# Causal block attention and a gated FFN on one core: a third piece with seven quarter products, plain maxima over the scores, low words on GpSimd

## The chip, the core and the metric

The kernel runs on one core of a Trainium2 chip. The metric is the device time in microseconds. Three runs of the kernel before took 951.97, 952.34 and 953.7 us; the median is 952.34.

## The reference

```python
scores = scale * np.matmul(q, k.transpose(0, 1, 3, 2))     # scale = 1/8
mask = block_i >= block_j                                  # blocks of 64 positions
scores = np.where(mask, scores, -1000000000.0)
scores = scores - np.max(scores, axis=-1, keepdims=True)
attn = np.exp(scores)
attn = attn / (np.sum(attn, axis=-1, keepdims=True) + 1e-09)
x = np.matmul(attn, v)                                     # heads side by side: 4608 x 512
...
h = x @ w_in                                               # 512 x 2048
g = h * np.clip(h + 3.0, 0.0, 6.0) / 6.0
out = g @ w_out                                            # 2048 x 512
```

There are 8 batches, 8 heads, 576 positions and head size 64; all inputs and outputs are float32.

## The kernel before

**Words.** A float32 operand is split into a high and a low float16 word (`nc.scaled` makes the high word, a multiply and subtract the low one), and a product is three float16 products: high x high, high x low, low x high. TensorE works with 64 output rows per matmul, two of them side by side on the two halves of the array.

**Attention.** Two heads make a pair (n = 0 to 31). Pairs 0 to 3 are computed in float32. For the others `s_group(n, g)` handles three blocks of 64 query rows (g = 0 to 2): it writes the scores of a block and all its keys into a bank of PSUM (`s`), and `to_softmax` lets VectorE copy the bank with a negative factor into the SBUF tile `p` and find the row minimum on the way, in one custom instruction and one that reads its accumulator. ScalarE takes the exponential of `p` in place, with the row sums; `st` holds minima, sums and their reciprocals. Then the high word of `p` times the reciprocal goes to `phl` on ScalarE or VectorE, and its low word by a `scalar_tensor_tensor` on VectorE (lines 1147 to 1158). A transposing DMA brings `phl` to `pT`, which `pv_group` multiplies with the words of V. Three PSUM buffers of tag s are shared by scores, pv and small statistics.

**FFN.** The 4608 tokens are cut into 13 pieces of at most 384 columns (numbers 0 to 12). A piece takes 16 slices f: the first layer makes h, ScalarE and VectorE make g from it, and the second layer adds g times `wout` into PSUM (`o`). In pieces of `STR` (line 56) the first layer is computed by a fast scheme with seven products of quarter matrices instead of eight (`h_pair`); it needs sums and differences of weights, made once by `w_comb`, and of x (`x_comb`). In pieces of `SO` (line 57) the second layer works so too (`g_pair`, `o_pair`); `t_comb` makes its tables once, from tiles `tr` and `tw` into room found by `t_homes`.

**Order.** Nothing here waits its turn by source order. `Recorder` collects every operation with its alternatives (`nc.add` gets a list of engines), and `ORDER`, a packed table of numbers, gives the order in which they are issued and the engine of each; `SLOTS` picks the buffer of each tile. So all instructions of an engine run in the order of the table, and they all carry line 423 in the profile.

Of the kernel before, what the change touches and what calls it, by code (L numbers as in the profile page):

```python
# [8 lines left out]
F16 = mybir.dt.float16  # L9
# [8 lines left out]
P = 128  # L18
# [38 lines left out]
SO = (11, 12)  # L57
# [21 lines left out]
    "c-l>Q1zaNC_qQS{Dvi0Rlyrl-X(u3IZra_oZrk0pZg+QgcXxMpcmL02pWpj=hvCLK-#GWqAk3~ghHbra)#^2C*O9O`!>rbC*obr4"  # L79
    "w0Vnj|A7Nsx&4S@9@%rSRK{}m=ZF-13Bha7)@|GUhQtT#*tu)BKrXaZdF<J{Z-2spgNF_uIeP54Hk^XD96G#NucI1#VuM3{$BY;i"  # L80
    "5_aO`Deu!~lxNSKpM2pWEi0mUT=o>Ry!??pqYDe#OG=9(qsPW|PBlg~#i-|Ns+RXz(9w5MbyrZJU3Xi>!j{&=X*KIMY_xDoN-it6"
    "uU)Y+r=f92@9tG~d#2OJ?@UQuJ!9sq1B^|(DsyjK-^bj0@Xgz_{p+_m9JzhxmZQ_L#cK{7Upsrw&A)iUw_o44o1HoP;OB(j=kDIS"
    "|IYj<?cv134)*7%pDui!g!yu%{_5t-Ted#?<7ja)<Lmot>6aXa`#gW~(s#+yWv{$n{~%HP1BhhLz|8)0Kj3Wq9KCFvoLxRTNoDdr"
    "%oBEx1`Qsn7?7C2QU(rmb#{wa(XnjzbcUrzT;r*er^gjO>DzDe<KQeIZ(hbzX;8A2yi_)9{Df@dip-{vi4ny`lSCzA375kcj2L-1"
    "yt!snN?zoU(PL&NrRuKaF3K+m3SOL+6Qv*97CmL<{#h}x#|*RU8>cF+wzMv3Dk~2?6BZJ>blLj$Yj9z%AFrrXTZeUYEmv!%byjWI"
    "xUaXmc4GJQIdwe^FQ(5RpW0Msd*Y<#*YC-v56pd7f8of{M}I!S#ku(S$-zUD{@yS%zZC!F^1P>*&u_ZppS_yDdyn?(%eSjn^{h!q"
    "tf^gVadVvw*0O=Q?e&ijtgTx%Z~tcXJ*oMpQpI-POQE&2PPx_g&Vyrzx4!$)v%lBy0WJjMxbc18Pw(SaI$_Yv+jj;J={NM=Fr2qG"
    "ynT6xD}BbS`?@nLR!+;!Ti_2xFv<qTC2)OL`S=Cs4J4}l&fY7DNduEp@^@V=C`_KWJ2Gm%vGYj!)Yxka7aYsHe)M>GT2WTTNKxgO"
    "(WAx|Z@jd5OE#~nx@6Pkh#_B7_w3F1CXBgoaRh($n(Ys|POe>dVr%qc!M^XaML$lZ9yoY<$DFx`4*&f1`_Hzaw}dxtzFGM8_WBKf"
    "@8sMZzxeLGclRGWd=#+=!^*aQe?4cyB))(vUXnW?udhp=e*Gia_5lN3-Ja~%m^p}-axVEsNou5${DMMj*|3RE-Q_%6bEfJ@R&^+j"  # L90
    "estM0ONR0j!OrTr4W2mI&yz&H@!{C#j~*MNhkH{TMmv7-qFxCIeDQM7V4v8Ac`>j2gI;f{RV)}Y_QVK_;E*t<ku>McqvF;#rZnqU"
    "zJm{It6?TKE#0YU@~zu-Tc%9Cvm?V#tJ_*s_UiK5%q#Pc-(5GZ{N968r_Y>SAO5i7@}tU@KlN1`+8#eS_t$LaQ+07xfAjko-1%MY"
    "nR_idW?6J%ySgt~O_<m-X)@OG!o}X{HYaVLS<g8-W%typv-eo`wd=PJPw=#|rta^5;2_bfWYA!m@1ZzK{ITOF7Lu}aj6R2t40-+L"
# [12 lines left out]
    "Dk2lFU#wbmv%2O|ZR5%rO*2<rKC^Jmjqd(E7B_G09yV+C$L8~O0^yuJb1$5|a<x7qbHVD(+=GYiUO&8d?bfX99A55?dGq(Fm3eEA"
    "jEvG~Z{0q+<yg2_)N=36fm0IQ1HBY(>y5;Rk0wohy#M4-BR@(e|N3IG;bru;{Iqn1%Ja$4r^h{FzJ0Iw5j$egv*(+x4WDw~{O8~k"
    "8N=>)W&YZ1=JLCIxc5zp)h#M*Q`ShIvdYn8va7tUhuHVwtRMAY;B8koU%I=4W88ub3v2)U_3^FWTIc5<uq8erw7RCD$;o*m<55fF"
    "w(Sp}`Z0Ix+`Dgi;G)*VB=|mKg$1z>1&2I~TzB_gL19sGNqj<La#HfRh}#ER3X59Xa@vo)JnDM?*l}ZCM`v@&^B1WiQhx64iM#IX"
    "CmT{yr%|YT-o2+69~OULyb5$XaWXjM^@N^zrOe*x<JqT9&zNax74YUQ%RPuD2@N}AKmRP}T$k4P@za;{vu4k^5Z-;`vyjUZ`Og(c"  # L110
    "f4!)7vBNuP_}{LZJDWM_BqKDA5tpxMuU^xC|1qI|WYn0kZ4*lbeeaD+`#Gu98aHxu%&5sze*Lx?AN!!pHa#OVD|^Sz-BV|RuJq5`"
    "c{2H_(?k9ilvg~AyL-Q`etu(RQ?retCA?#hQnjaQz%HkOPoCC18l3N;(=R3v4W5sUd#iKySy|(*ELnPH|AE6^%Z@C!S+Vl$s-v%_"
    "pF964ckR0M2Rk=7ZhO{x=x4*P*Q?hYJF)F})W%KEUqrr)&ino6Z|%vp_O6)Nj!v^TZ+o}C`?h&Y1mW8E&&~tB5J@w(fB48?UUGD~"
    "K<?`9)9*TE#3)<49I5Q<`yV|cr%`ERN6Qr#l`6b_t|!ZDG23CF#}!KpzS|OaPQtL^ee?4BxnAz?<Z`3$puuCN_Um63AD1|!d#HCo"
    "l8^A_t-{;M&V9;#Q`1t$PZ*HCYRziDs-^w`ShOFLCQlsL<7z&AN=5Co%4u#GLD(fmU43su$MV3ScKQk~{3v}@efY@Qb!ClB!AE!V"
    "w)QT2vq4>2Gh^oKt0A*i&JJC_k-llq-un;UFWR?*b9c@-?&OD$j?H~na(cn^ooAZQZr<{C+t#9D-nDb*cl|kjd*O$VpSJ%sGrw>#"
    ";c?=f&&jN>-|p=H^8E*!FF5(@#Lvzr*WvGY@m;yF)Zkt+4l~~3)C7^3=`pVWr+E6z#&*74pr<sbps+>--yy#*Yqa+FriA04hb2vP"
# [24 lines left out]
    "U04wvb3Jy%$P=eV9qyIRoO5aJyyJg<|6ROb;hZH$mYrE@X@wO{IkX&}!7iRYdiLCn(PKm^>nq}$ztkG-)NmX9q35>_<F4u?hCIv#"
    "x|vii5ZapC;RzS1L=uhcK(w@HyK}5Ak=?94a5iPWeikH|Lixh;C1t*-d<9p<d-d}&vm(;g4zDON2Hp1ZA6L5N2VeYpa9FhDn#?GV"
# [1797 lines left out]
```

## Time and profile before

| What | Value |
|---|---|
| median of three runs | 952.34 us |
| time of the profiled execution | 951.95 us |
| its span | 950.2 us |
| TensorE (PE) busy | 942.8 us |
| VectorE (DVE) busy | 860.0 us |
| ScalarE (ACT) busy | 722.0 us |
| GpSimd (POOL) busy | 98.3 us |
| mean granted TensorE clock | 0.999 of 2.4 GHz |

The span runs from the first to the last instruction; the time of the execution has 1.75 us more around it. Busy time of an engine that runs ahead of the others costs nothing; what counts is where TensorE has to wait. Matmul ends in the profile are modelled, so the distance from one start to the next tells more than a duration.

### The profile page before, as it was taken

Reading aid. Unit: us, or ns where it says so; the run is one execution under the profiler, and the core shown is the slowest. Engines: PE = TensorE matmul, PEld = TensorE weight load, DVE = VectorE, ACT = ScalarE, POOL = GpSimd, SP = SyncE. Lnnn points to the kernel's source line nnn. Section 1 sums busy time; section 2 is a strip of 40 time slices with the busy share of each in tenths; the row PEclk is TensorE's granted clock in tenths of the full one; section 3 lists DMA queues with packets and bytes.
Section 4 is the critical chain, followed back from the end, with each engine's and each line's share of the span. In section 5 each row is a group of like instructions: output and inputs, shape, how many; then the busy total and the mean of one; then the engine's idle time right before and its main releaser. Section 6 shows DMA issues by size and latency. Waiting matters only on the chain.

```text
span 950.2 us, 34711 instructions
## 1 busy us (share of the span) xinstructions
PE 942.8 (99%) x14108; PEld 686.3 (72%) x14108; DVE 860.0 (91%) x2526; ACT 722.0 (76%) x1791; POOL 98.3 (10%) x283
## 2 busy tenths in 40 slices
PE   9999999999999999999999999999999999999998
PEld 7777777766677766666667666666666667789998
DVE  5988999999999999999999999999899998999987
ACT  6989898888988878888788878778665356676662
POOL 1443101100000000110000010100000102000000
PEclk9999999999999999999999999999999999999999
DMA  7877699989999999999999899986785000000001
GB/s 211 280 246 213 125 178 169 180 166 181 167 189 168 179 188 162 183 189 181 165 201 181 169 165 180 179 162 121 127 128 106 2 2 36 2 35 4 14 26 36
DMA packets 390704, 132.93 MB, mean 140 GB/s; under 512 B 373264, under 2 KB 376592, under 8 KB 390544
## 3 DMA queue, kind: packets, MB, share of 16 engines
q1 hardware_dynamic: 389456, 129.87, 71.7%
q8 instruction: 110, 1.80, 0.8%
q10 hardware_dynamic: 1088, 0.85, 0.3%
q14 instruction: 50, 0.41, 0.1%
HBM read 45.09 MB, written 9.44 MB: 57 GB/s over the span
## 4 chain that ended last, share of the span: by engine, by line
PE 97%; DMA 1%; DVE 1%; ACT 0%; issue 0%; SPq 0%; DVEq 0%
PE o L423 37%; PE h L423 30%; PE m L423 9%; PE s L423 7%; PE pv L423 6%; PE pf L423 1%; PE sf L423 1%; PE pt L423 1%; DMA qkT<-qks 1%; PE pr L423 1%; PE gm L423 0%; DMA qf<-in_q_dram 0%; PE warm L423 0%; PE o_1b L423 0%; PE o_2b L423 0%; PE o_0b L423 0%
## 5 line engine op out<-in xcount | busy, mean ns | idle before, releaser
L423 PE MATMUL o<-wout,g 128*64 128x512 f16 (+2 forms) x2760 | 346.5, 378 | 0.0
L423 PE MATMUL h<-x,win 128*64 128x384 f16 (+2 forms) x3568 | 330.1, 318 | 0.0
L423 PEld LDWEIGHTS <-win 128*64 128x64 f16 (+1 forms) x4432 | 231.7, 110 | 81.3 <-issue 1.7
L423 PEld LDWEIGHTS <-g 128*64 128x64 f16 x2784 | 154.0, 110 | 98.6
L423 DVE SCALAR_TENSOR_TENSOR phl<-p,st,phl 128x64 f16<-128x64 f32 (+4 forms) x364 | 154.9, 447 | 4.2 <-ACT phl L423 2.3
L423 ACT ACTIVATE p<-p,st 128x192 f32<-128x192 f32 (+8 forms) x252 | 139.1, 553 | 22.7 <-DVE st L423 20.7
L423 DVE CUSTOM_DVE_ANT_0 p<-s,none,esc 128x64 f32<-128x64 f32 (+7 forms) x252 | 119.9, 486 | 14.6 <-PE s L423 11.2
L423 ACT ACTIVATE r<-h,eg,sh 128x384 f32<-128x384 f32 (+1 forms) x176 | 101.5, 591 | 40.2 <-PE h L423 33.9
L423 ACT ACTIVATE phl<-p,st 128x512 f16<-128x512 f32 (+5 forms) x173 | 97.2, 582 | 11.2 <-DVE st L423 6.1
L423 PE MATMUL s<-qkT 128*64 128x512 f16 (+7 forms) x1120 | 98.5, 287 | 0.8 <-DMA qkT<-qks 0.8
L423 DVE SCALAR_TENSOR_TENSOR g<-r,g 128x384 f16<-128x384 f32 (+1 forms) x160 | 86.2, 546 | 3.8 <-ACT g L423 3.0
L423 DVE SCALAR_TENSOR_TENSOR r<-r,eg,h 128x384 f32<-128x384 f32 (+1 forms) x144 | 84.2, 586 | 5.8 <-ACT r L423 4.5
L423 ACT ACTIVATE g<-r 128x384 f16<-128x384 f32 (+1 forms) x117 | 58.3, 503 | 18.2 <-PE o L423 11.3
L423 PEld LDWEIGHTS <-qkT 128*64 128x64 f16 x1120 | 53.4, 110 | 25.1 <-DMA qkT<-qks 1.0
L423 PEld LDWEIGHTS <-vhl 128*64 128x64 f16 x1344 | 58.4, 110 | 13.4
L423 PE MATMUL pv<-pT,vhl 128*64 128x192 f16 (+2 forms) x1344 | 67.2, 233 | 0.0
L423 ACT ACTIVATE hf<-m 128x192 f32<-128x192 f32 x90 | 28.5, 327 | 36.9 <-PE m L423 31.9
L423 PEld LDWEIGHTS <-ws 128*64 128x64 f16 x1152 | 52.0, 110 | 4.1
L423 ACT ACTIVATION_READ_ACCUMULATOR p<-p,st 128x1 f32 x252 | 47.7, 189 | 0.0
L423 DVE SCALAR_TENSOR_TENSOR qks<-qk,rs_q,qks 128x576 f16<-128x576 f32 x56 | 46.8, 838 | 0.9 <-ACT qks L423 0.6
L423 PE MATMUL m<-x,ws 128*64 128x192 f16 x864 | 46.8, 246 | 0.0
L423 PE MATMUL m<-x,win 128*64 128x192 f16 x768 | 41.4, 246 | 0.4 <-DVE hf L423 0.4
(229 smaller groups left out, 1414.1 us busy)
## 6 DMA issues: line engine op xcount, KB each, us to landing
vx<-vhl SPq DMA_DIRECT2D x56, 160.0 KB, 3.4
vnat<-in_v_dram SPq DMA_DIRECT2D x63, 128.0 KB, 3.5
qk<-in_k_dram SPq DMA_DIRECT2D x28, 288.0 KB, 4.4
qk<-in_q_dram SPq DMA_DIRECT2D x28, 288.0 KB, 3.9
out_dram<-osb SPq DMA_DIRECT2D x29, 256.0 KB, 2.8
rawo<-in_moe_w_out_dram SPq DMA_DIRECT2D x13, 512.0 KB, 4.9
x<-in_moe_w_in_dram SPq DMA_DIRECT2D x9, 512.0 KB, 5.5
rawi<-in_moe_w_in_dram SPq DMA_DIRECT2D x6, 512.0 KB, 4.8
```

The source lines that it names most:

```text
L423: getattr(eng, method)(*args, **kw)
```

## The change

Three things change, and with them the tables `ORDER` and `SLOTS`.

1. `SO` gets piece 10, so its second layer uses `g_pair` and `o_pair`. The tables of `t_comb` are made before piece 10, after those of `w_comb`, and lie partly behind the tables `ws` in tiles of the attention (`more`).
2. For blocks 0 to 7 of each pair VectorE takes a plain maximum of the score bank; the maximum is scaled and negated by any of three engines, and ScalarE's exponential reads the bank in PSUM and writes `p`. Block 8 keeps the custom instruction.
3. `low_word` gives each low word of P two ways: the one on VectorE, or two instructions on GpSimd (multiply `p` in place, subtract the high word). In turn the sums and differences of `w_comb`, `x_comb` and `t_comb` are VectorE's alone.

```diff
-SO = (11, 12)
+SO = (10, 11, 12)
...
 ORDER = (
-    "c-l>Q1zaNC_qQS{Dvi0Rlyrl-X(u3IZra_oZrk0pZg+QgcXxMpcmL02pWpj=hvCLK-#GWqAk3~ghHbra)#^2C*O9O`!>rbC*obr4"
...
+    def low_word(out, x, r, high):
+        nc.add([
+            ("vector", "scalar_tensor_tensor", (out, x, r, high), dict(op0=ALU.mult, op1=ALU.subtract)),
+            ("gpsimd", [
+                ("tensor_scalar", (x, x, r, 1.0), dict(op0=ALU.mult, op1=ALU.mult)),
+                ("tensor_tensor", (out, x, high), dict(op=ALU.subtract)),
+            ]),
+        ])
...
+                    if g * GB + ii < NB - 1:
+                        x = col[ii]
+                        nc.vector.tensor_reduce(st[:, x:x + 1], ps[:, o:o + c1 - c0], axis=AX.X, op=ALU.max)
+                        src[ii] = ps[:, o:o + c1 - c0]
+                        mine.append(ii)
+                        continue
...
+            nc.add([
+                ("vector", "tensor_scalar", (st[:, whole], st[:, some_], sc, 1.0), dict(op0=ALU.mult, op1=ALU.mult)),
+                ("scalar", "activation", (st[:, whole], st[:, some_], AF.Copy), dict(scale=sc)),
+                ("gpsimd", "tensor_scalar", (st[:, whole], st[:, some_], sc, 1.0), dict(op0=ALU.mult, op1=ALU.mult)),
+            ])
...
+                if ii in src:
+                    prs[ii] = attp.tile([P, NJ * P], F32, tag="p", bufs=NPB, name=f"p{n}_{g * GB + ii}")
+                    nc.scalar.activation(
+                        prs[ii][:, :nk], src[ii], AF.Exp, bias=st[:, 10 + col[ii]:11 + col[ii]],
+                        scale=up, accum_out=st[:, 4 + col[ii]:5 + col[ii]],
+                    )
+                    continue
...
-                nc.vector.scalar_tensor_tensor(
-                    units(u0 + 1, full), cols(full), r, units(u0, full), op0=ALU.mult, op1=ALU.subtract
-                )
+                low_word(units(u0 + 1, full), cols(full), r, units(u0, full))
...
-        rest += [[va[:, i]] for i in range(4)]
+        rest += [[more[3], more[5]], [more[4], va[:, :1]], [more[6], va[:, 1:2]], [more[7], va[:, 2:]]]
```

How the order moves, at three places. The first is VectorE in group 1 of pair 10 (blocks 3 to 5; a name such as s10_1_2_0 is the bank of pair 10, group 1, third block, and p10_5 the tile of block 5). Before:

```order
L423 ISA p10_5_919,st10_1_913<-s10_1_2_0_918,none_99,esc10_835 128x384
L423 ISA st10_1_913 128x1
L423 ISA p10_3_915,st10_1_913<-s10_1_0_0_914,none_99,esc10_835 128x256
L423 ISA st10_1_913 128x1
...
L423 ISA p10_4_917,st10_1_913<-s10_1_1_0_916,none_99,esc10_835 128x320
L423 ISA st10_1_913 128x1
...
L423 RECIPROCAL st10_1_913<-st10_1_913 128x3
...
L423 SCALAR_TENSOR_TENSOR phl10_1_920<-p10_4_917,st10_1_913,phl10_1_920 128x64
...
L423 SCALAR_TENSOR_TENSOR phl10_1_920<-p10_3_915,st10_1_913,phl10_1_920 128x2x128
...
L423 SCALAR_TENSOR_TENSOR phl10_1_920<-p10_5_919,st10_1_913,phl10_1_920 128x3x128
...
L423 SCALAR_TENSOR_TENSOR phl10_1_920<-p10_4_917,st10_1_913,phl10_1_920 128x2x128
```

After, the same group:

```order
L432 TENSOR_REDUCE st10_1_914<-s10_1_2_0_919 128x1
L432 TENSOR_REDUCE st10_1_914<-s10_1_1_0_917 128x1
...
L432 TENSOR_REDUCE st10_1_914<-s10_1_0_0_915 128x1
...
L432 TENSOR_SCALAR st10_1_914<-st10_1_914,esc10_836 128x1
...
L432 RECIPROCAL st10_1_914<-st10_1_914 128x3
L432 TENSOR_SCALAR phl10_1_921<-p10_4_918,st10_1_914 128x2x3x64
L432 SCALAR_TENSOR_TENSOR phl10_1_921<-p10_4_918,st10_1_914,phl10_1_921 128x2x128
...
L432 SCALAR_TENSOR_TENSOR phl10_1_921<-p10_5_920,st10_1_914,phl10_1_921 128x3x128
```

Three custom instructions with their accumulator reads have become three reduces and one tiny scale, and of the four low words of the group (the SCALAR_TENSOR_TENSOR rows into phl10_1) two are left here.

The second is GpSimd around the same group. Before, it only clears padding and forms sums:

```order
L423 TENSOR_SCALAR st10_0_891<-st10_0_891 128x3
L423 MEMSET phl9_1_862 128x128
L423 MEMSET phl10_1_920 128x128
L423 MEMSET p10_4_917 128x64
L423 MEMSET p10_8_939 128x64
L423 MEMSET p10_6_938 128x64
L423 TENSOR_SCALAR st10_2_934<-st10_2_934 128x3
```

After:

```order
L432 TENSOR_SCALAR p10_0_894<-p10_0_894,st10_0_892 128x64
L432 TENSOR_TENSOR phl10_0_897<-p10_0_894,phl10_0_897 128x64
...
L432 TENSOR_SCALAR st10_1_914<-st10_1_914 128x3
L432 MEMSET p10_4_918 128x64
L432 TENSOR_SCALAR p10_4_918<-p10_4_918,st10_1_914 128x64
L432 TENSOR_TENSOR phl10_1_921<-p10_4_918,phl10_1_921 128x64
...
L432 TENSOR_SCALAR st10_2_935<-st10_2_935,esc10_836 128x1
L432 TENSOR_SCALAR p10_3_916<-p10_3_916,st10_1_914 128x256
L432 TENSOR_TENSOR phl10_1_921<-p10_3_916,phl10_1_921 128x2x128
...
L432 MEMSET phl10_1_921 128x128
```

The low words have come here, as pairs of a multiply in p10 and a subtraction into phl10, between the small instructions on st that VectorE and ScalarE wait for.

The third is TensorE where piece 10's second layer begins (m10 are first-layer products of piece 10, o10 its second layer, one row of each group shown). Before:

```order
L423 MATMUL m10_2_5_2283<-vnat_101,ws2_2244 64x192
...
L423 MATMUL o10_2_2281<-wout_86,g10_0_2265 64x512
...
L423 MATMUL o10_2_2281<-wout_86,g10_1_2267 64x512
...
L423 MATMUL o10_0_2279<-wout_86,g10_0_2265 64x512
...
L423 MATMUL m10_3_7_2290<-vnat_101,ws3_2247 64x192
```

After, at the first place with several products in a row:

```order
L432 MATMUL o9_0_1987<-wout_86,g9_15_2117 64x512
...
L432 MATMUL o10_4_2323<-tq_2269,gs10_0_1_2304 64x128
...
L432 MATMUL o10_4_2323<-wout_86,gr10_0_2302 64x128
...
L432 MATMUL o10_3_2322<-tq_2269,gs10_0_0_2303 64x128
...
L432 MATMUL m10_3_7_2330<-x2_83,win_85 64x192
```

Matmuls of 512 columns from g10 and wout have become products of 128 and 256 columns (those of 128 are for the last 64 of a quarter's 192 tokens), which read the tables tq and the words gr and gs of g_pair.

## Rows read from the trace of the kernel before

**Rows 1.** the page, busy time of each engine (share, instructions), and the chain by engine
```profile
PE 942.8 (99%) x14108; PEld 686.3 (72%) x14108; DVE 860.0 (91%) x2526; ACT 722.0 (76%) x1791; POOL 98.3 (10%) x283
...
PE 97%; DMA 1%; DVE 1%; ACT 0%; issue 0%; SPq 0%; DVEq 0%
```

**Rows 2.** timeline of TensorE at 696 us: start, length, operation, operands, count
```profile
696.65 2.11 PE L423 MATMUL o<-wout,g 128*64 128x512 f16 x18
698.59 0.87 PE L423 MATMUL s<-qkT 128*64 128x512 f16 x8
```

**Rows 3.** busy us (instructions) of PE, PEld, DVE, ACT, POOL in four stretches; clock, DMA
```profile
100.00:400.00 300.00, 299.14 (x4258) 211.36 (x4256) 278.65 (x892) 257.65 (x658) 25.38 (x98) 1.00 0.98 171
400.00:700.00 300.00, 300.00 (x4063) 198.72 (x4061) 276.16 (x850) 240.39 (x615) 25.91 (x103) 1.00 0.95 167
700.00:800.00 100.00, 100.00 (x1408) 68.45 (x1406) 91.54 (x206) 52.94 (x109) 11.71 (x14) 1.00 0.27 53
800.00:900.00 100.00, 99.65 (x2058) 88.38 (x2056) 93.08 (x222) 66.67 (x148) 0.35 (x1) 1.00 0.03 11
```

**Rows 4.** timeline of TensorE at 850 us, second layer of piece 11
```profile
850.52 0.33 PE L423 MATMUL o<-tq,gr 128*64 128x128 f16 x6
...
850.86 0.49 PE L423 MATMUL o<-wout,gr 128*64 128x256 f16 x6
...
851.51 0.33 PE L423 MATMUL o<-wout,gr 128*64 128x128 f16 x6
```

**Rows 5.** busy us of DVE, ACT, POOL, instructions that touch tw alone
```profile
780.00:880.00 100.00, 21.92 (x44) 9.50 (x17) 2.27 (x2) 1.00 0.05 19
```

**Rows 6.** VectorE's groups: operands, form, count, busy us, mean ns, idle before
```profile
L423 DVE CUSTOM_DVE_ANT_0 p<-s,none,esc 128x64 f32<-128x64 f32 (+7 forms) x252 | 119.9, 486 | 14.6 <-PE s L423 11.2
...
L423 DVE CUSTOM_DVE_ANT_0 p<-s,none,esc 128x64 f32<-128x64 f32 x56 | 15.6, 278 | 1.6 <-PE s L423 1.4
...
L423 DVE DVE_READ_ACCUMULATOR2_ANT st<- 128x1 f32 x320 | 26.6, 83 | 0.0
...
L423 DVE TENSOR_TENSOR hf<-m,hf 128x192 f32<-128x192 f32 x72 | 24.5, 353 | 10.0 <-PE m L423 7.5 <-ACT hf L423 1.3 <-ACT gs L423 0.5
...
L423 DVE TENSOR_SCALAR x<-pv 128x384 f16<-128x384 f32 x3 | 1.6, 539 | 0.0
...
L423 DVE SCALAR_TENSOR_TENSOR esc<-pw_q 128x1 f32<-128x1 f32 x28 | 4.6, 165 | 0.0
...
L423 DVE SCALAR_TENSOR_TENSOR phl<-p,st,phl 128x64 f16<-128x64 f32 x140 | 39.2, 284 | 2.4 <-ACT phl L423 1.4
...
L423 DVE SCALAR_TENSOR_TENSOR phl<-p,st,phl 128x512 f16<-128x512 f32 x56 | 42.1, 753 | 0.5 <-ACT phl L423 0.2
...
L423 DVE SCALAR_TENSOR_TENSOR g<-r,g 128x384 f16<-128x384 f32 x144 | 80.6, 567 | 2.8 <-ACT g L423 2.1
```

**Rows 7.** GpSimd's groups by form
```profile
L423 POOL TENSOR_SCALAR qks<-qks 128x576 f16<-128x576 f16 x26 | 20.9, 802 | 71.7 <-DVE qks L423 43.0 <-ACT qks L423 22.9 <-DVE pp L423 3.4
...
L423 POOL TENSOR_SCALAR st<-st 128x3 f32<-128x3 f32 x40 | 10.8, 271 | 230.7 <-ACT p L423 202.7 <-DVE r L423 12.6 <-issue 11.3
...
L423 POOL TENSOR_TENSOR tr<-wout 128x512 f32<-128x512 f16 x1 | 1.2, 1218 | 0.1
...
L423 POOL TENSOR_TENSOR rs<-hf 128x192 f32<-128x192 f32 x1 | 0.7, 712 | 110.9 <-DVE hf L423 110.9
```

**Rows 8.** ScalarE's exponential, all widths together, from the page
```profile
L423 ACT ACTIVATE p<-p,st 128x192 f32<-128x192 f32 (+8 forms) x252 | 139.1, 553 | 22.7 <-DVE st L423 20.7
```

**Rows 9.** timeline at 744 us, GpSimd and VectorE
```profile
744.49 2.18 POOL L423 TENSOR_TENSOR wr<-win 128x1024 f32<-128x1024 f16 x1 [13.52 <-DVE wq L423]
...
744.71 2.37 DVE L423 SCALAR_TENSOR_TENSOR g<-r,g 128x384 f16<-128x384 f32 x1
```

**Rows 10.** tiles g and s: minimum, median, maximum ns of a VectorE group
```profile
L423 DVE SCALAR_TENSOR_TENSOR g<-r,g x160: 350/552/2366, 122.9 to 835.2; 128x384 f16<-128x384 f32 x144, 128x192 f16<-128x192 f32 x16
...
L423 DVE CUSTOM_DVE_ANT_0 p<-s,none,esc x252: 264/479/752, 107.1 to 715.9; 128x64 f32<-128x64 f32 x26, 128x128 f32<-128x128 f32 x17, 128x512 f32<-128x512 f32 x16, 128x256 f32<-128x256 f32 x15
```

More of the change, by code (lines that the diff above doesn't have):

```diff
@@ L84 @@
[L84 to L93, printed above, removed]
@@ L1075, in s_group @@
         T = qkT[n]
-        sc = esc[n]
+        sc, up = esc[n][:, 0:1], esc[n][:, 1:2]
         banks = (
@@ L1155, in s_group @@
             if half:
-                nc.vector.scalar_tensor_tensor(
-                    ph[:, last, BLK:], pr[:, nk - BLK:nk], r, ph[:, last, :BLK], op0=ALU.mult, op1=ALU.subtract
-                )
+                low_word(ph[:, last, BLK:], pr[:, nk - BLK:nk], r, ph[:, last, :BLK])
             if g == 2:
@@ L1299 @@
     sw = {}
+    more = {}
     homes = []
@@ L1308, in plus, with minus @@
     def plus(out, a, b):
[L1309 removed]
+        nc.add([(e, "tensor_tensor", (out, a, b), dict(op=ALU.add)) for e in ("vector",)])
+    def minus(out, a, b):
+        nc.add([(e, "tensor_tensor", (out, a, b), dict(op=ALU.subtract)) for e in ("vector",)])
     def w_comb(c):
[L1313 to L1314 removed]
+        wr = [ffp.tile([P, 2, NH], F32, tag="stage", bufs=NST_B, name=f"wr{c}_{j}") for j in range(2)]
+        for j, r in enumerate(wr):
+            plus(r, win[:, c, 2 * j:2 * j + 2, 0], win[:, c, 2 * j:2 * j + 2, 1])
         o = attp.tile([P, 4, 2, P], F32, tag="phl1", bufs=1, name=f"wq{c}")
[L1316 to L1320 removed]
+        a11, a12, a21, a22 = (wr[j][:, :, i * P:(i + 1) * P] for i in range(2) for j in range(2))
+        plus(o[:, 0], a21, a22)
+        minus(o[:, 1], o[:, 0], a11)
+        minus(o[:, 2], a11, a21)
+        minus(o[:, 3], a12, o[:, 1])
         tag = SW_TAGS[c]
@@ L1453, in t_comb @@
         o = attp.tile([P, 4, NM], F32, tag="phl1", bufs=1, name=f"tw{c}")
-        def minus(out, a, b):
-            nc.add([(e, "tensor_tensor", (out, a, b), dict(op=ALU.subtract)) for e in ("vector", "gpsimd")])
         minus(o[:, 0], b12, b11)
@@ L1746, in ffn_step @@
             pc, f = divmod(done1, NFT)
-            if pc == SO[0] and f == 0:
-                was = nc.key, nc.cls, nc.grp
-                nc.cls = "a"
-                homes.extend(t_homes())
-                for c in range(NCH):
-                    nc.grp = 3200 + c
-                    t_comb(c)
-                nc.key, nc.cls, nc.grp = was
             if pc in STR and f == 0:
@@ L1765, in ffn_step @@
                         w_comb(c)
+                nc.key, nc.cls, nc.grp = was
+            if pc == SO[0] and f == 0:
+                was = nc.key, nc.cls, nc.grp
+                nc.cls = "a"
+                homes.extend(t_homes())
+                for c in range(NCH):
+                    nc.grp = 3200 + c
+                    t_comb(c)
                 nc.key, nc.cls, nc.grp = was
```

340 lines of the change are left out of this document (181 added, 159 removed).

## The prediction

> **What bounds the kernel now.** I read the busy shares and the chain of waits first. TensorE is busy for 942.8 of 950.2 us, and the chain that ended last is 97% TensorE [rows 1]. A busy TensorE is not yet one that streams, so I looked at its timeline: 18 matmuls of 512 columns start at 696.65 and the next group at 698.59 [rows 2]. Two matmuls of 64 output rows run side by side, so that is nine pairs in 1.94 us, 0.2156 us a pair; 512 columns at 2.4 GHz are 0.213. It streams, and the granted clock is 1.00 in every stretch read [rows 3]. Between 100 and 900 us it is idle for 0.86 and 0.35 us and nowhere else [rows 3]. So the time falls by the columns taken off TensorE and rises by waits that do not exist today. The engine nearest to causing such waits is VectorE: 278.65 + 276.16 = 554.8 us of the 600 between 100 and 700, 92%, and 93% between 800 and 900 [rows 3]. ScalarE has 83% there and GpSimd 9%.
>
> **The change, part by part.**
>
> *Piece 10's second layer.* Removed: 16 slices x 3 row tiles x 3 word products x 2 halves = 288 matmuls of 512 columns, 144 pairs. Added: 8 slices x 7 products x 3 word products x 2 halves = 336 of 256 columns and as many of 128, 168 pairs of each. The pieces that already work so show the prices: two rows of six matmuls, six pairs of 256 columns, from 850.86 to 851.51, 0.108 us a pair, and two rows of 128 columns from 850.52 to 850.86, 0.057 a pair [rows 4]. So 144 x 0.2156 = 31.0 us go and 168 x (0.108 + 0.057) = 27.7 come: **-3.3 us**, all on the path, since TensorE is the path. The order confirms that nothing else of TensorE's work changes size; its first 904 matmuls are the same ones in the same order, so the start keeps its cost.
>
> What feeds these products is not free. The combined tables of the second-layer weights are built once in both kernels, but before piece 10 now, no longer before piece 11: 22 us of VectorE work on tw, which lie between 780 and 880 us today [rows 5], move in front of the first quarter product, into a stretch where VectorE is busy for 91.5 of 100 us [rows 3]. I cost it at nothing because VectorE comes to that stretch with room from the stretch before (next part); if that cover is gone, TensorE waits at piece 10's first o products.
>
> *Plain maxima.* 224 of the 252 custom instructions go (eight of nine blocks, 28 head pairs; the 64-column start of block 8 stays): 119.9 us less 28 x 0.278 = 112 us of VectorE, and 224 accumulator reads at 0.083, 18.6 us [rows 6]. In their place stand 224 max-reduces from PSUM, which the trace does not show at these widths. From above they cost what the custom ones did, 112 us. From below, other operations that read PSUM give 0.353 us at 192 and 0.539 at 384 columns [rows 6], or 0.167 + 0.97 per thousand columns; the eight widths sum to 2304, so 28 x (8 x 0.167 + 2.235) = 100 us. I take 100, since a reduce reads the same and writes one column. The sign and scale then need 168 tiny instructions: 47 on VectorE (0.165 each as esc [rows 6], 7.8 us), the others on ScalarE and GpSimd.
>
> The price of this part is elsewhere. A score bank in PSUM came free after VectorE's one instruction; now it is held until ScalarE's exponential has read it: a scale (0.165 to 0.271 us, [rows 6, 7]) and an exponential (0.553 on the mean [rows 8]), some 0.75 us more for each of 224 banks, 168 us. Three such banks over 600 us are 1800 us of bank time, so this is 9% of it. What is queued behind: the score matmul that takes the bank next, and on TensorE all that stands after it. From below it costs nothing (today's PSUM waits, for VectorE, show only as a fraction of 0.86 us in 300); from above all 168 us in a row. I take the low end plus 0.7 us, since o, h and pv products stand between the score groups and most banks have two others beside them.
>
> *Low words on GpSimd.* The order puts 191 of 364 there: 88 of 64 columns, 29 of 128, 27 of 256, 25 of 384, 22 of 512. VectorE's price is 0.284 at 64 and 0.753 at 512 [rows 6], on a line between: 25.0 + 10.2 + 13.1 + 15.5 + 16.6 = 80 us off VectorE. GpSimd needs two instructions. The one-input kind is 0.271 at 3 columns and 0.802 at 576, the two-input kind 0.712 at 192 and 1.218 at 512 [rows 7]; on these lines a low word is 0.84 us at 64 and 1.96 at 512, together 223 us. GpSimd goes from 51 to some 280 of 600 us, not a bound; the transposing DMA that follows starts about a microsecond later, and today TensorE waits for none of these DMAs between 400 and 700 us [rows 3].
>
> Sum for VectorE between 100 and 700: 555 - 112 - 18.6 + 100 + 7.8 - 80 = **452 us**, 75% (464 with the dear reduce). But the two engines get in each other's way. At 744.71 a VectorE instruction that has two SBUF inputs and a usual time of 0.552 us took 2.37: it ended when GpSimd's two-input instruction of 744.49 did [rows 9, 10]. This is the risk in the change. Such waits are seldom today: over its 144 instances the 384-column form of that group has a mean of 0.567 us [rows 6] against the group's median of 0.552 [rows 10], 2.6% over; on 860 us of VectorE that is 22 us, for 98 us of GpSimd, 0.23 per us. With 0.23 x 223 = 51 us VectorE comes to 503 us, 84%, still below today's 92%. And the 1.8 us wait cost TensorE nothing: it is 100.00 busy between 700 and 800 [rows 3].
>
> [...]
>
> Sum: the profiled execution took 951.95 us, its span 950.2 and 1.75 around it; 950.2 - 3.3 + 0.7 = 947.6, and 1.75 makes 949.35. That execution lies 0.4 us under the median of 952.34. I predict **949.5 us**.
>
> **The rivals.**
>
> *Rival 1: the score banks and the late tables give the gain back.* For: 0.75 us more per bank, and the 22 us of tables that come forward. Against: 9% of bank time, and VectorE's 100 us of new room ahead of piece 10. If each of the 224 banks costs TensorE 0.015 us, that is 3.3 us in place of my 0.7: 952.0 us, no change. Its range is 950.4 to 954.3.
>
> *Rival 2: GpSimd stops VectorE until VectorE is the bound.* The place is the stretch from 100 to 700 us, where the low words are. For: the instance at 744.71, a wait of 1.8 us for 2.18 us of GpSimd, 0.83 per us. Against: 0.23 per us on the mean, and what reads the scores in PSUM was never held: the longest of 252 custom instructions took 0.752 us [rows 10]. VectorE then needs 452 + w x 223; it bounds from about 96% of 600, 576 us (the busiest stretch has 93%, and TensorE loses 0.35 us in it [rows 3]), that is w = 0.56. At w = 0.6 it needs 586, and 586/0.96 = 610 us for the stretch, 10 us more: 960 us. At w = 0.83 it would be 637/0.96 = 664, 64 us more. Below 0.56 this rival costs little.
>
> *Rival 3: more than the columns.* The freed VectorE time also takes away what is left of waits in the middle (0.86 + 0.35 us [rows 3]) and of the transition into the f16 part: 946.5 to 947.5 us. For: VectorE's share goes down by 8 points. Against: nearly nothing is left to win.
>
> **How the numbers follow.** Forecast (947.5 to 950.4) 0.55; rival 1, 0.22; rival 2 or a milder form of it above 954.3, 0.16; rival 3, 0.07. About 0.2%, 1.9 us, can be told from no change here: faster means below 950.4, slower above 954.3. So faster is 0.55 + 0.07 = 0.62, same 0.22, slower 0.16. The range reaches from 946.8, inside rival 3, to 956.5, past rival 1 and into mild forms of rival 2, and leaves out its dear end; the forecast's own range is 947.5 to 950.4.
>
> **What the profile after would show.** Right: TensorE idle below about 2 us between 100 and 900, 336 pairs of 256 and 128 columns in piece 10, VectorE's busy time between 100 and 700 near 500 us, GpSimd's near 280, and a reduce at 512 columns near 0.66 us. Rival 1: waits of s or pv matmuls for ScalarE's p, or of o for the tables, that add up to 3 us. Rival 2: VectorE above 95% with low words and g words two or three times their usual time, and TensorE waiting for r or hf. My sum is wrong if the 128-column pairs cost more than 0.057 us in piece 10, if the reduce costs more than the custom instruction did, or if TensorE's waits in the middle are above 2 us.

## The result and the profile after

The changed kernel takes **964.17 us**, the median of four runs (961.0 to 965.41), beside 952.46 us of the kernel before in the same comparison: a ratio of 1.0116, with a 95% interval from 1.0088 to 1.0144. Forecast were 949.5 us and 946.8 to 956.5. It became slower, by 11 to 12 us, and in a second comparison on another chip by the same (964.81 beside 952.62, 1.0126 from 1.0093 to 1.0158).

The page of the kernel after, busy times and the chain by engine, answers to [rows 1]:

```profile
PE 945.0 (98%) x14492; PEld 731.8 (76%) x14492; DVE 859.8 (89%) x2211; ACT 728.2 (76%) x1819; POOL 386.4 (40%) x764
...
PE 35%; DVE 5%; DMA 3%; ACT 2%; issue 1%; POOL 1%; SPq 0%; DVEq 0%; ACTq 0%; POOLq 0%
```

VectorE is no busier than before, and its share has even gone down. The chain of waits reaches back over the whole span before; after, it can be followed only to 497 us (its shares add up to 47%), so 35% is not to be set against 97%. But in that half VectorE, the transfers, ScalarE and GpSimd have 11 of the 47, where they had 2 of the whole. The windows of the kernel after answer to [rows 3] (columns as there):

```profile
100.00:400.00 300.00, 295.33 (x4180) 220.21 (x4178) 272.83 (x740) 254.38 (x650) 136.56 (x299) 1.00 0.97 169
400.00:700.00 300.00, 297.87 (x4013) 207.62 (x4011) 267.20 (x709) 251.23 (x655) 140.69 (x300) 1.00 0.96 170
700.00:800.00 100.00, 98.40 (x1349) 76.88 (x1345) 96.17 (x199) 60.06 (x123) 24.05 (x35) 1.00 0.22 44
800.00:900.00 100.00, 97.67 (x2311) 95.81 (x2308) 91.72 (x189) 57.16 (x129) 36.05 (x46) 1.00 0.04 12
```

TensorE's idle time appears in every stretch: 4.67, 2.13, 1.60 and 2.33 us, where it was 0.86, 0, 0 and 0.35. The clock is 1.00 throughout. What TensorE waited for, first in the kernel before (whole view), then in the one after (the rows beyond the first four that name an engine's result):

```profile
PE warm L423 <- DVE zero L423: 1.1, 1, 1.1
PE s L423 <- DMA qkT<-qks: 0.8, 1, 0.8
PE qt L423 <- DMA qf<-in_q_dram: 0.6, 1, 0.6
PE m L423 <- DVE hf L423: 0.4, 1, 0.4
```

```profile
PE h L432 <- DVE r L432: 2.7, 4, 1.5
...
PE m L432 <- DVE hf L432: 1.4, 3, 0.6
PE s L432 <- DMA qkT<-qks: 1.3, 1, 1.3
PE s L432 <- ACT p L432: 1.1, 1, 1.1
...
PE pv L432 <- DMA pT<-phl: 0.8, 2, 0.5
PE pv L432 <- ACT p L432: 0.6, 1, 0.6
```

No single wait has come; there are many, for VectorE, for ScalarE and for the transfers behind them. Since this view leaves out short ones and busy matmuls hide some, I also summed them from the starts: each matmul is given its columns at 2.4 a nanosecond (a pair of 512 columns takes 0.2156 us and a pair of 128 takes 0.057, so 384 columns more take 0.159), and what a start comes later than that, by more than 25 ns, is a wait. The columns came out as forecast: the page counts 384 matmuls more (288 fewer of 512 columns, 336 more each of 256 and 128), which is **3.8 us less at this rate, and 3.3 us less at the distances between starts**. In the first 100 us both kernels wait about equally long. After 100 us the waits are 6.3 and 22.7 us: 16.4 us more, where 0.7 had been set down. (These sums depend by some 1 to 2 us on how matmuls that run side by side are paired; a difference of that size between two runs tells nothing.)

How one of them comes about is seen in the timeline of the kernel after at 372 us (start, length, engine, operation):

```profile
371.97 0.69 POOL L432 TENSOR_SCALAR p<-p,st 128x512 f32<-128x512 f32 x1 [1.45 <-ACT phl L432]
...
372.31 2.18 DVE L432 SCALAR_TENSOR_TENSOR g<-r,g 128x384 f16<-128x384 f32 x2 [0.33 <-ACT g L432]
...
372.74 1.34 POOL L432 TENSOR_TENSOR phl<-p,phl 128x512 f16<-128x512 f32 x1
...
375.03 0.96 POOL L432 TENSOR_TENSOR phl<-p,phl 128x384 f16<-128x384 f32 x1
...
375.27 1.28 DVE L432 SCALAR_TENSOR_TENSOR phl<-p,st,phl 128x512 f16<-128x512 f32 x1
...
376.58 0.46 ACT L432 ACTIVATE p<-s,st,esc 128x128 f32<-128x128 f32 x1 [1.31 <-DVE phl L432]
...
377.18 0.35 PE L432 MATMUL s<-qkT 128*64 128x384 f16 x2 [1.14 <-ACT p L432]
```

Two g words that usually take 0.55 us each last 2.18 together, until 0.41 us after GpSimd's subtraction of 372.74 is done; a low word of VectorE that usually takes 0.753 [rows 6] takes 1.28 beside the subtraction of 375.03. It comes late with them, so ScalarE's next exponential, which needs its p buffer, waits 1.31 us for it, and a score matmul waits 1.14 us for the bank that this exponential reads. The held bank is the way by which this wait reaches TensorE.

### The profile page after: what moved, and what is told of

Same layout as the page of the kernel before. It is cut to its first block, busy times and chain, and to the rows that moved or that the text cites. A ratio compares the mean times of both kernels' runs of the same rounds, so it can differ in the third digit from the quotient of the medians.

```text
span 963.6 us, 35713 instructions
## 1 busy us (share of the span) xinstructions
PE 945.0 (98%) x14492; PEld 731.8 (76%) x14492; DVE 859.8 (89%) x2211; ACT 728.2 (76%) x1819; POOL 386.4 (40%) x764
## 5 line engine op out<-in xcount | busy, mean ns | idle before, releaser
L432 PE MATMUL o<-wout,g 128*64 128x512 f16 (+3 forms) x2472 | 313.6, 378 | 0.5 <-DVE osb L432 0.5
L432 POOL TENSOR_SCALAR p<-p,st 128x64 f32<-128x64 f32 (+4 forms) x191 | 112.8, 591 | 165.9 <-ACT phl L432 88.1
L432 ACT ACTIVATE p<-s,st,esc 128x192 f32<-128x192 f32 (+6 forms) x224 | 130.7, 586 | 24.5 <-POOL st L432 11.1
L432 POOL TENSOR_TENSOR phl<-p,phl 128x64 f16<-128x64 f32 (+4 forms) x191 | 123.0, 644 | 15.9
L432 DVE TENSOR_REDUCE st<-s 128x1 f32<-128x256 f32 (+7 forms) x224 | 97.0, 449 | 13.5 <-PE s L432 11.6
L432 PE MATMUL s<-qkT 128*64 128x64 f16 (+7 forms) x1120 | 100.0, 287 | 3.2 <-DMA qkT<-qks 1.3
L432 DVE SCALAR_TENSOR_TENSOR phl<-p,st,phl 128x64 f16<-128x64 f32 (+4 forms) x173 | 93.0, 547 | 3.7 <-ACT phl L432 2.6
L432 POOL TENSOR_TENSOR rs<-hf 128x192 f32<-128x192 f32 x36 | 28.2, 797 | 145.6 <-DVE hf L432 145.6
L432 POOL TENSOR_SCALAR st<-st,esc 128x1 f32<-128x1 f32 (+1 forms) x61 | 24.1, 397 | 73.3 <-DVE st L432 70.9
L432 PEld LDWEIGHTS <-gs 128*64 128x64 f16 x1152 | 53.0, 110 | 0.4
```

Source lines behind the costliest of these rows:

```text
L432: getattr(eng, method)(*args, **kw)
```

## The experiments

GpSimd's *reading* of long tiles is one thing, its slowness another, and the banks, the tables and VectorE's load are others again; the expectations name the theories L (low words), M (banks) and T (tables and sums around piece 10). All runs beside the kernel before; "waits" is TensorE's sum after 100 us as above, in the profiled run; "held" the time by which VectorE's instructions between 100 and 700 us exceed the median of their own form without GpSimd beside them (over 0.1 us each).

| run | us | ratio, 95% interval | waits | held |
|---|---|---|---|---|
| before | 952.46 | | 6.3 | 7.0 |
| after | 964.17 | 1.0116, 1.0088 to 1.0144 | 22.7 | 35.4 |
| e1_before_low | 983.64 | 1.0351, 1.0319 to 1.0382 | 36.5 | 21.9 |
| e8_after_nolow | 982.13 | 1.0315, 1.0290 to 1.0340 | 37.7 | 3.7 |
| e7_after_wide | 979.21 | 1.0290, 1.0273 to 1.0307 | 36.4 | 36.0 |
| e2_after_zero | 957.53 | 1.0059, 1.0036 to 1.0082 | 14.5 | 6.1 |
| e3_after_memset | 955.38 | 1.0039, 1.0020 to 1.0058 | 11.7 | 9.2 |
| e9_after_depmem | 956.44 | 1.0055, 1.0038 to 1.0071 | 14.2 | 5.5 |
| f4_depmem_last | 956.34 | 1.0045, 1.0028 to 1.0062 | 13.0 | 5.6 |
| e11_after_halfmem | 961.61 | 1.0101, 1.0079 to 1.0123 | 17.9 | 33.1 |
| e12_after_shortmax | 961.09 | 1.0097, 1.0074 to 1.0120 | 17.8 | 36.1 |
| e4_after_nomax | 963.32 | 1.0130, 1.0111 to 1.0148 | 20.1 | 36.2 |
| e13_after_notab | 962.48 | 1.0114, 1.0093 to 1.0135 | 20.1 | 34.8 |
| e10_depmem_notab | 956.57 | 1.0049, 1.0032 to 1.0066 | 12.9 | 6.3 |
| e6_after_pmdve | 972.60 | 1.0222, 1.0202 to 1.0241 | 29.4 | 36.2 |
| f1_depmem_nomax | 958.26 | 1.0054, 1.0031 to 1.0077 | 12.0 | 5.9 |
| f2_depmem_pmsham | 953.84 | 1.0018, 1.0005 to 1.0032 | 10.8 | 6.3 |
| f3_depmem_pm_nomax | 954.52 | 1.0017, 1.0000 to 1.0034 | 11.5 | 6.1 |

**Low words moved, one part alone (e1, e8).** e1 is the kernel before, with the same 191 low words sent to GpSimd; e8 the kernel after, with all of them on VectorE:

```diff
+            if o.low and LOWS[o.low[0] - 4] >> 2 * o.low[1] + (o.low[2] == 64) & 1:
+                o.eng = "gpsimd"      # e1
+            if o.low and not 9998 <= o.low <= 9999:
+                o.eng = "vector"      # e8
```

> The kernel before in its own order, with the 191 low words that the change gives to GpSimd on GpSimd; nothing else of the change. Theory L (the low words on GpSimd make most of the 12 us: GpSimd and VectorE hold each other, and what TensorE waits for comes late): 8 to 13 us above the kernel before, about 962 us, and TensorE's waits between 100 and 700 us grow from about 1 to 8 us or more. Theory M (the score banks, held until the exponential has read them, make it): within 2 us of the kernel before, 950 to 954 us. Theory T (the tables and quarter sums around piece 10 make it): also within 2 us.

> The changed kernel with all low words on VectorE, at the same places of its order; piece 10 and the plain maxima stay. Theory L: most of the loss goes, 951 to 955 us (VectorE's 540 us between 100 and 700 us lose the 45 us of being held and gain 80 us of low words, about 575 of 600, so that some wait for VectorE may remain). Theories M and T: 961 us or more, since the banks are held and the tables are made as in the changed kernel.

Both are more than 30 us slower than the kernel before. e1 lies far above the 8 to 13 us of theory L; e8 misses L's 951 to 955 us and, though M and T said 961 us or more, lies 18 us above the kernel after, which neither explains. The low words on GpSimd cost much in the old order, and taking them back costs much in the new one. In e1 a second cost shows, in what VectorE waited for:

```profile
DVE p L428 <- POOL phl L428: 40.0, 37, 3.1
```

In that order VectorE writes the next p, and waits 40 us for buffers that GpSimd's low words still read. In e8 the windows are:

```profile
100.00:400.00 300.00, 291.25 (x4094) 219.50 (x4094) 274.68 (x806) 248.95 (x631) 33.79 (x116) 0.99 0.92 166
400.00:700.00 300.00, 293.26 (x3897) 215.83 (x3893) 274.83 (x780) 247.73 (x643) 28.41 (x112) 1.00 0.92 166
```

Nothing holds VectorE any more (3.7 us), it is busy for 92%, and TensorE loses 15.5 us in these 600. The kernel before had VectorE at 92% too, and lost 0.86 [rows 3]. So the share doesn't tell. That the order was laid out for other durations is the likely reason; no run tried an order made for e1 or e8.

**No reading by GpSimd (e2, e3, e9, f4).** Low words on GpSimd become memsets: one; three or four; those behind a one-column subtraction that keeps the waits for p and the high word; and that subtraction once more at the end, so that p stays held as long:

```diff
-                ("tensor_scalar", (x, x, r, 1.0), dict(op0=ALU.mult, op1=ALU.mult)),
-                ("tensor_tensor", (out, x, high), dict(op=ALU.subtract)),
+                ("tensor_tensor", tuple(first(a) for a in (out, x, high)), dict(op=ALU.subtract)),
+            ] + [("memset", (out, 0.0), {})] * (1 if out.shape[-1] * (len(out.shape) == 3 and out.shape[1] or 1) == 64 else 2) + [
+                ("tensor_tensor", tuple(first(a) for a in (out, x, high)), dict(op=ALU.subtract)),   # f4
```

> The changed kernel, in which each of the 191 low words on GpSimd is one memset of the low word to zero in place of multiply and subtract: these low words are left out of the result. VectorE keeps only its 171 others. Theory L: TensorE's waits after 100 us fall from about 18 us to 5 or less, 948 to 951 us, as predicted for the change. Theory M: 960 us or more, the banks are held as before. Theory T: the 6 us between 700 and 950 us stay, about 957 us.

> The changed kernel, in which each of the 191 low words on GpSimd is three or four memsets of the low word in place of multiply and subtract, so that GpSimd is busy about as long per low word but reads nothing: these low words are left out of the result. Theory L by sharing (VectorE's and GpSimd's instructions hold each other at the SBUF): VectorE's held instructions go from 159 to near the 37 of the kernel before and the time to 953 us or less. Theory L by delay (the low word, and with it the transposing DMA and GpSimd's small instructions, simply come later on a slow engine): 960 us or more, with hardly any held VectorE instruction. Theory M: 960 us or more.

> The changed kernel, in which each low word on GpSimd is a subtraction of one column (it waits for p and the high word as before, and holds the same place in GpSimd's queue) and two or three memsets of the whole low word, together about as long as multiply and subtract last when nothing holds them: these low words are left out of the result. Theory L by sharing (GpSimd's reading instructions hold VectorE's and are held by them): as with memsets alone, 953 to 957 us, and held VectorE instructions between 100 and 700 us stay near 31, not 99. Theory L by delay (GpSimd's slow answer, its place in a queue behind waits for p): 961 us or more, as the changed kernel. In between, both.

> The changed kernel, in which each low word on GpSimd is a one-column subtraction, one or two memsets, and the one-column subtraction again (these low words are left out of the result). Unlike the kernel with one subtraction ahead of the memsets (956.4 us), it lets the buffer of p go only at the end of GpSimd's work on it, as the changed kernel does. If the long reading itself (sharing) costs the time: 955 to 957.5 us again. If the p buffers, held longer by a slower engine, cost it: 960 us or more.

> The changed kernel itself, beside the one above on the same chip: 961 to 965.5 us, and by either theory what the one above is to be compared with.

All four come to 955 to 957.5 us, whatever GpSimd's busy time (102 us between 100 and 700 in e2, 242 in e9, where the kernel after has 277), its waits and the p buffers: on one chip f4 took 956.34 and f5, the kernel after once more, 964.81. e9, f4 and f5 came as forecast for sharing; e2 missed theory L's 948 to 951 us and e3 its 953, so something beside the low words is left. So the reading makes 6 to 8 us; GpSimd's delay and the buffers don't show. VectorE's groups, first of the kernel after, then of e9 (busy us, mean ns):

```profile
L432 DVE SCALAR_TENSOR_TENSOR g<-r,g 128x384 f16<-128x384 f32 x128 | 76.4, 600 | 3.9 <-ACT g L432 3.3
...
L432 DVE SCALAR_TENSOR_TENSOR phl<-p,st,phl 128x64 f16<-128x64 f32 x52 | 19.6, 379 | 1.2 <-ACT phl L432 0.9
L432 DVE TENSOR_REDUCE st<-s 128x1 f32<-128x512 f32 x28 | 19.1, 684 | 1.8 <-PE s L432 1.8
...
L432 DVE SCALAR_TENSOR_TENSOR so<-pw_v,egm 128x1 f32<-128x1 f32 x32 | 8.4, 262 | 0.0
```

```profile
L432 DVE SCALAR_TENSOR_TENSOR g<-r,g 128x384 f16<-128x384 f32 x128 | 71.0, 558 | 5.4 <-ACT g L432 4.7
...
L432 DVE TENSOR_REDUCE st<-s 128x1 f32<-128x512 f32 x28 | 19.2, 687 | 2.9 <-PE s L432 2.8
...
L432 DVE SCALAR_TENSOR_TENSOR phl<-p,st,phl 128x64 f16<-128x64 f32 x52 | 14.5, 283 | 0.8 <-ACT phl L432 0.6
...
L432 DVE SCALAR_TENSOR_TENSOR so<-pw_v,egm 128x1 f32<-128x1 f32 x32 | 5.6, 175 | 0.0
```

What has two SBUF inputs was held, even over one column (262 against 175 ns); the reduce from PSUM was not (684 against 687 ns at 512 columns). Of the kernel after's 35.4 us, 29.0 lie in SCALAR_TENSOR_TENSOR with two SBUF inputs and the other 6.3 in TENSOR_SCALAR with one (20 instructions). Where one of two inputs lies in PSUM (r<-r,eg,h and x<-pv,x, 99 instructions beside a GpSimd that reads long tiles) none was held.

**Part of the low words (e7, e11).** e7 has the 117 narrow low words back on VectorE, e11 makes them memsets; the 74 wide ones stay in both:

```diff
+            if o.low and not 256 <= o.low <= 9999:
+                o.eng = "vector"                              # e7
+            ("gpsimd", sham if n < 200 else real),            # e11
```

> The changed kernel with the 117 low words of 64 and 128 columns back on VectorE, at the same places of its order; the 74 of 256 to 512 columns stay on GpSimd. VectorE gets some 35 us more of its own between 100 and 700 us, GpSimd some 110 us less. If the number of encounters makes the cost, the time falls, to 957 to 962 us; if VectorE has no time to give back in this order (as with all low words back, 982 us), it rises to 968 to 976 us.

> The changed kernel in which only the 117 low words of 64 and 128 columns are a one-column subtraction and memsets (these are left out of the result); the 74 of 256 to 512 columns are computed on GpSimd as before. The narrow ones have 46% of GpSimd's time for low words. If the holds go with GpSimd's reading time: 959 to 962 us, about half of the 8 us between the changed kernel and the one with all of them replaced. If the wide ones alone hold VectorE: 963 us or more; if the number of encounters decides: 957 us.

e7 says what e8 did, and more than forecast (979.21 us for 968 to 976): this order has no place on VectorE for them. e11 is near the middle as expected, though the time held hardly falls (35.4 to 33.1 us), so the total held doesn't set the time; its interval reaches into that of the kernel after, and it decides little.

**VectorE freed without touching GpSimd (e12).**

```diff
-nc.vector.tensor_reduce(st[:, x:x + 1], ps[:, o:o + c1 - c0], axis=AX.X, op=ALU.max)
+nc.vector.tensor_reduce(st[:, x:x + 1], ps[:, o:o + BLK], axis=AX.X, op=ALU.max)
```

> The changed kernel in which each of the 224 maxima reads 64 columns of its bank and not all of them (the maximum over the other columns is left out). VectorE loses about 224 x (0.447 - 0.28) = 37 us, near the 35 us by which GpSimd holds it between 100 and 700 us; GpSimd's work and the sharing stay. If TensorE loses its time because VectorE runs late: 953 to 957 us. If it loses it because GpSimd's own results come late: 961 us or more.

The windows of e12, and then of e9:

```profile
100.00:400.00 300.00, 295.91 (x4182) 216.08 (x4182) 251.45 (x741) 254.50 (x656) 140.80 (x300) 1.00 0.98 171
400.00:700.00 300.00, 299.19 (x4085) 208.77 (x4081) 248.31 (x718) 252.38 (x657) 139.69 (x302) 1.00 0.94 169
```

```profile
100.00:400.00 300.00, 295.35 (x4184) 220.84 (x4182) 259.20 (x742) 255.83 (x657) 121.57 (x442) 1.00 0.95 171
400.00:700.00 300.00, 299.76 (x4095) 198.27 (x4093) 259.34 (x718) 252.55 (x656) 120.03 (x445) 1.00 0.95 169
```

e12 has 40 us of VectorE less than the kernel after and gains at most 3 (by the ratios 2, with intervals that overlap); e9 has 19 us more than e12 and is faster than it (the intervals don't touch). So it isn't the sum of VectorE's time that was lost; what remains is single instructions at the wrong moment. Whether those of VectorE or GpSimd's own, which were held too (a multiply that takes 0.311 us at least took up to 1.312), stays open: by its expectation the 961.09 us speaks for GpSimd's late results, while e2 and e9, 140 us of GpSimd apart, speak against them.

**The banks (e4, f1).** The exponential takes a zero for its bias:

```diff
-                        prs[ii][:, :nk], src[ii], AF.Exp, bias=st[:, 10 + col[ii]:11 + col[ii]],
+                        prs[ii][:, :nk], src[ii], AF.Exp, bias=none[:, 0:1],
```

> The changed kernel, in which the exponential of blocks 0 to 7 takes zero for its bias and so waits no longer for reduce and scale; reduces and scales are still made, and the subtraction of the maximum is left out. A score bank is free earlier by the scale and by the wait for it. Theory M (held banks): 955 us or less. Theory L: 960 to 963 us; only the 3.4 us that TensorE waits for ScalarE's reading of the banks can go, and what GpSimd's low words delay stays.

> The kernel with one-column subtractions and memsets for GpSimd's low words, and besides the exponential with zero for its bias, which waits no longer for reduce and scale: low words and the subtraction of the maximum are left out of the result. It was 956.4 us without this edit, 4.8 above the kernel before, with 10 us of TensorE's waits between 100 and 700 us (5 in the kernel before). If the banks held for the exponential make these (theory M, for what the low words leave): 951 to 953 us and 6 us of waits there. If not: 955 to 957 us.

Nothing is gained, with reading GpSimd or without (963.32 us where theory M had 955 or less, 958.26 where it had 951 to 953). What reduce and scale add to the time that a bank is held falls as a cause. That ScalarE's exponential reads the bank at all, and so holds it while it waits for its own p buffer as at 377.18, is the same in every run and was not tried.

**Around piece 10 (e13, e10, e6, f2, f3).** e13 and e10 make the 32 differences of the tables memsets; e6 puts the 72 sums of `g_pair` on VectorE; f2 and f3 make them one-column operations and memsets on GpSimd:

```diff
-        minus(o[:, 0], b12, b11)
...
+                ("gpsimd", "memset", (o[:, i], 0.0), {}),                              # e13, e10
...
             nc.add([(e, "tensor_tensor", (out, a, b), dict(op=op)) for e in ("vector", "gpsimd")])
+            nc.ops[-1].low = 1        # e6, and where the engine is read:
+            if o.low:
+                o.eng = "vector"
...
-            nc.add([(e, "tensor_tensor", (out, a, b), dict(op=op)) for e in ("vector", "gpsimd")])
+                    ("tensor_tensor", (out[:, :1], a[:, :1], b[:, :1]), dict(op=op)),  # f2, f3
+                    ("memset", (out, 0.0), {}),
+                    ("memset", (out, 0.0), {}),
```

> The changed kernel with the 32 differences of the second-layer tables as memsets on GpSimd (the tables are left out of the result) and nothing else: by theory T 960 to 962.5 us, 1.5 to 4 us below the changed kernel, all of it after 730 us; otherwise 963.5 to 965 us.

> The kernel with one-column subtractions and memsets for GpSimd's low words, and besides the 32 differences of the second-layer tables (0.413 us each on VectorE, 13 us between 730 and 827 us) as memsets on GpSimd: low words and tables are left out of the result. Theory T (the tables make the waits around piece 10's first quarter products): TensorE's waits between 800 and 850 us, 3.2 us in every kernel with the change so far, fall below 1.5 us, and the time is 1.5 to 3 us under the kernel without this edit (956.4), 953 to 955 us. If the tables don't matter there, 3.2 us and 956 us stay.

> The changed kernel with the 72 sums and differences of the quarter words in pieces 10 to 12 on VectorE instead of GpSimd (0.35 us each instead of 0.80, 25 us more of VectorE's time, 57 us less of GpSimd's, all after 700 us). Theory T as sharing around piece 10: the 6 us of waits after 700 us shrink, 960 to 962 us. Theory T as VectorE's own shortage there (the tables came to a stretch where it is busy for 96 of 100 us): 966 to 975 us. Theory L says nothing of these stretches.

> The kernel with one-column subtractions and memsets for GpSimd's low words, and besides the 72 sums and differences of the quarter words (pieces 10 to 12) as one-column operations and two memsets on GpSimd: low words and these sums are left out of the result, and nothing that GpSimd reads at length is left after 700 us. If GpSimd's sharing with VectorE also makes the 3 us of waits between 800 and 850 us: they fall below 1.5 us, and the time from 956.4 to 953 to 955 us. If they come from the two banks that the first-layer products of piece 10 have left beside its six accumulators, and from ScalarE's and VectorE's queues behind them: they stay above 2.3 us, 955.5 to 957 us.

> Both edits together (low words, the sums of the quarter words and the subtraction of the maximum are left out of the result). If sharing and held banks are all that stands between the kernel and the forecast: 949 to 951.5 us, TensorE's waits after 100 us near 6 us as before the change. If something else remains (order of the work, transfers): 953 us or more.

Without the tables' differences, about half of VectorE's 24 us on the tables, the waits between 800 and 850 us go only from 3.2 to 2.8 us (e9 to e10), and neither ratio moves beyond its interval. e13's 962.48 us still lies at the upper edge of theory T's range: a microsecond or two is not excluded, the bulk of the 12 is. Sums on VectorE cost 8 to 10 us more, as its own shortage there had said (966 to 975). Without GpSimd's reading of them f2 comes to 1.0018, 0.4% under e9, and the intervals don't touch. Their stretch from 800 to 900 us, in e6 and in f2:

```profile
800.00:900.00 100.00, 93.65 (x2177) 90.83 (x2173) 91.72 (x221) 55.73 (x124) 0.00 (x0) 1.00 0.06 17
```

```profile
800.00:900.00 100.00, 99.00 (x2364) 97.94 (x2361) 85.36 (x198) 56.54 (x127) 38.81 (x132) 1.00 0.05 13
```

f3 adds nothing to f2 (954.52 us, the case in which something else remains). What is left, some 2 us above the kernel before and 4 above the forecast, isn't settled. f2's waits between 800 and 850 us are 2.2 us, between the 1.5 and 2.3 of its two cases, nearly all before first-layer products (m); `bank()` leaves the first-layer products of piece 10 only the h banks from its third slice pair on, since its second layer now takes three s banks. That this makes them was argued, not tried. Nor were piece 10 alone, with an order of its own, or any version that keeps the whole computation and beats both kernels.

## Why the prediction was wrong, step by step

- *Piece 10's columns, -3.3 us*: right. In the kernel after six pairs of 256 columns take 0.65 us and three of 128 take 0.17, 0.108 and 0.057 a pair as in [rows 4]:

```profile
820.96 0.33 PE L432 MATMUL o<-wout,gr 128*64 128x128 f16 x6
821.13 0.82 PE L432 MATMUL o<-tp,gs 128*64 128x256 f16 x12
821.78 0.82 PE L432 MATMUL o<-wout,gr 128*64 128x256 f16 x12
```

- *Tables at nothing*: right within what e13 and e10 can tell, though by luck, not for the reason given: the room on VectorE wasn't there (96% from 700 to 800 us), and e6 shows it. *The sums of `g_pair`* stand in no term: the new order has GpSimd make 72 of them (56 us, after 700 us), where the old one had it make 1 [rows 7], and f2 prices their reading at 3 us.
- *Reduces*: 0.684 us at 512 columns for 0.66, 97 us in all for 100. Right. *Banks at 0.7 us*: not contradicted by e4 and f1; rival 1's causes, as far as they were tried, make a microsecond or two at most.
- *Low words on GpSimd*: 236 us for 223, right in size, as were 277 us of GpSimd for 280. Holds are less than forecast: (35.4 - 7.0) / 226 us more of GpSimd is 0.13 per us, not 0.23, and the kernel before itself has 7.0 us for 51, 0.14; a group's mean over its median was no measure of them. (The instruction of 744.71 ended at 747.08, not with GpSimd's of 744.49 but 0.41 us after it.) And yet VectorE between 100 and 700 us is 540 us, not 503. Two things were wrong in that sum. The order gave VectorE 17 more high words of p and 21 more of g, 16 us, which I had not counted. And I took whole groups off a busy time in which they overlap: the groups of the kernel before add up to 663 us where its windows have 555 (after, 624 for 540), and an accumulator read starts 75 ns before the end of its custom instruction, so 18.6 us of such reads were hardly there to win, as at 299.41 in the timeline of the kernel before:

```profile
299.41 0.74 DVE L423 CUSTOM_DVE_ANT_0 p<-s,none,esc 128x512 f32<-128x512 f32 x1
300.08 0.08 DVE L423 DVE_READ_ACCUMULATOR2_ANT st<- 128x1 f32 x1
```

- *The step that failed*: "still below today's 92%", and with it waits of +0.7 us. I took a hold of VectorE for a sum of time that fits as long as the share stays under 96%, a bound that no row gave: e8 lost 15.5 us at 92%, with hardly a hold. Every engine here runs the fixed list of its order, and what stands behind a held instruction comes late, as at 372 us, where TensorE's score matmul waited 1.14 us in the end; the longest hold between 100 and 700 us of the kernel after, of the low word at 194.20, is 0.97 us. The share stayed at 90% between 100 and 700 us, under today's 92%, and the waits after 100 us rose by 16.4 us, not 0.7. Taking GpSimd's reading of the low words away (e9) took 8.5 of these 16.4 back, and that of the sums too (f2) 11.9; where the other 4.5 come from stays open. The one hold in my rows, 1.8 us at no cost to TensorE [rows 9], stood where the next results had slack.
- *Rival 2* had the right mechanism and the wrong threshold: it was to cost little below 0.56 per us, and at 0.13 GpSimd's reading cost 6 to 8 us for the low words, and 9 of the 11 to 12 with the sums of pieces 10 to 12 (1.0116 to 1.0018).

## What to carry to other kernels

Here the low words given to GpSimd were paid for twice: with the 236 us that GpSimd spent on them, and with what VectorE ran beside its reading of SBUF. VectorE's instructions with two SBUF inputs were held for 29.0 us between 100 and 700 us, and the cost is to be looked for in what waits behind them, not in VectorE's busy share: the share went from 92% to 90%, while without that reading, in e9, TensorE waits 8.5 us less. In this kernel, whose order is fixed, moving the same work back cost more than leaving it (982.13 us in e8 and 979.21 in e7, beside 964.17); that a change of durations alone, even a relief, acts like a change of the order is how I read it, and no run shows it by itself. Before a share is called room, one run with a stand-in that keeps GpSimd's time and drops its reads tells what the room is worth.

## What the runs showed of the hardware

GpSimd's memsets held next to nothing: in e9 GpSimd is busy for 242 of 600 us, 138 of them in memsets of phl and 52 in one-column subtractions, and VectorE's held time is 5.5 us, under the 7.0 of the kernel before with 51 us of GpSimd; with 277 us, most of it multiplies and subtractions, it is 35.4. What memsets did hold was TENSOR_SCALAR. In e3, 256 of VectorE's SCALAR_TENSOR_TENSOR between 100 and 700 us met nothing but memsets, and none was held by 0.1 us; of 113 TENSOR_SCALAR that met nothing but memsets 20 were, for 4.4 us. One of them, over three columns, took 0.50 us, until the memset was done, where 0.23 is usual:

```profile
366.86 0.89 POOL L432 MEMSET phl<- 128x384 f16 x2
...
367.28 0.50 DVE L432 TENSOR_SCALAR st<-st,esc 128x3 f32<-128x3 f32 x1
```

GpSimd was held too: in the kernel after, its multiply over 64 columns takes 0.311 us at least, 0.517 on the mean of 88, and 1.312 at most. The 32 beside which VectorE ran nothing with two SBUF inputs take 0.324 us on the mean and 0.422 at most, the other 56 take 0.628 on the mean. By what means the two engines hold each other no run shows.
